# Building constants from the identity on VectorE, and turning x of one more batch on TensorE, in a fused attention and wave-MLP kernel

## The chip, the cores and the metric

The kernel runs on one core of a Trainium2 chip. A core has a matrix engine (TensorE, PE in the profile; its weight loads are shown apart as PEld), a vector engine (VectorE, DVE), a scalar engine (ScalarE, ACT), a pool engine (GpSimd, POOL) and a sync engine (SyncE, SP) that here only issues DMAs. Sixteen DMA engines move data between the memories. TensorE writes into PSUM, which has eight banks of 128 partitions by 512 float32; the other data lie in SBUF. Each engine runs its own instructions in order and waits for the others at semaphores. The metric is the device time of one execution in microseconds (us).

## The reference

Inputs are q, k and v of shape (8 batches, 8 heads, 576 positions, 64), and four weight matrices. Attention is computed twice, once on means of four positions and once in a narrow band; both are added, the heads are put side by side as x, and x goes through a wave MLP:

```python
q_d, k_d, v_d = (t.reshape(B, H, 144, 4, D).mean(axis=3) for t in (q, k, v))
out_up = np.repeat(softmax(q_d @ k_d.T / 8) @ v_d, 4, axis=2)
mask = np.abs(pos[:, None] - pos[None, :]) < 4
out_local = softmax(where(mask, q @ k.T / 8, -1e9)) @ v
x = (out_up + out_local).transpose(0, 2, 1, 3).reshape(8, 576, 512)

theta = x @ w_theta
y = w_tok_r @ (x * cos(theta)) + w_tok_i @ (x * sin(theta))
u = x + y
return u + relu(u @ w_ch)
```

## The kernel before

The work of a batch is cut into some forty small steps, each a Python generator, and the string `ORDER` names by one letter which step is emitted next; every engine runs its instructions exactly in that order. `BANKS` gives the PSUM bank of each TensorE step that writes one, and `ENGINES` says for five kinds of copies which engine makes each: p is POOL, v is VectorE, a is ScalarE. The order interleaves batches, so that the attention of one runs beside the MLP of an earlier one.

A batch goes through these steps (the letters are those of `ORDER`). **Inputs:** L loads k, q and v from SP into float32 staging tiles `st` (lines 217 and 220; thirteen items per batch, fifteen tiles in rotation); C casts them to bf16, on the engine that `ENGINES` names (line 124, as for all such copies). **Turns:** A turns k and q on TensorE (L287), a copies the result out of PSUM; d and e sum four positions of k and of q (L304; L316 on VectorE for batch 0, L321 and L322 on POOL for the others). **Pooled attention:** P scores (L369, L381), p their exponential (L388), U the pooled v as a matrix product with the pooling matrices `PU` (L335, L337), u its copy out, x spreads the last pooled rows over heads by the owner columns `own` (L350, on POOL), N the product with v (L401, L407), n its normalisation, Q and q its turn. **Band attention:** S scores (L455), s their exponential (L467), m the product with the 0-1 matrix `band` (L475, VectorE), O the product with v (L487), o and i its normalisation. **x:** T turns and t adds both attentions to x, with positions along the free axis (`xT`, L550). **MLP:** H and G multiply by the theta weights (L565, L583), h and g take sine and cosine on ScalarE (L572, L573, L590); X turns x on TensorE (L617) so that y can multiply it with sine and cosine (L633); J is the token mix (L658) with its residual j; K the channel product (L701) with its relu b; D the store.

Three parts matter for what follows.

**Constants** (step k, lines 144 to 193). The identity `ident` is made on POOL by a memset and an affine select. The matrices `band` (128 x 64), `pu0`, `pu1`, `pu4` (128 x 32 each) and `own` (128 x 4) are made on POOL too. `halves` fills a scratch tile with the value, cuts it by affine selects (two to four for each half of the partitions) and copies each half to its place.

**Weights** (step l). Twenty DMAs issued by POOL bring the weights and convert them to bf16 on the way: four pieces of theta (L251), six pieces each of the two token matrices (L249), four pieces of the channel matrix. V turns the token matrices on TensorE (L263) and v copies them out. The first mix of batch 0 needs all of them turned.

**x for the product.** In most batches X turns a batch's x by sixteen 128 x 128 transposes on TensorE into four PSUM banks, and y reads it from there. For the batches in `BY_QUEUE` (5, 6, 7) step M has SP issue two DMA transposes from SBUF to SBUF instead (L626); y then reads x from SBUF. In those batches `xT` is laid out in two separate parts, and the last piece of t is two instructions.

## Time and profile before

| | |
|---|---|
| runs shown | 236.91, 240.9 and 241.18 us; median 240.9 |
| the profiled execution | 238.6 us; span of its instructions 236.9 us |
| granted TensorE clock, mean | 0.997 |
| TensorE busy | 209.1 us, 88% of the span |
| VectorE busy | 195.1 us, 82% |
| ScalarE busy | 152.2 us, 64% |
| GpSimd busy | 90.5 us, 38% |
| moved by DMA | 49.05 MB, mean 207 GB/s |

The span runs from the first to the last instruction. An engine is busy while one of its instructions runs, whatever that instruction is worth; matmuls overlap one another, so a busy TensorE can still have slack. In a view by groups a row reads: line, engine, operation, what is written and read, shapes and count, then total and mean time, then idle time before them and what ended it. In a view by time a row begins with the start and the length in microseconds. In a row of waits three numbers follow the waiting instruction and its releaser: total, count and longest.

### The profile page before, as it was taken

What the parts mean: (1) busy time and instruction counts of PE and PEld (TensorE: products, weight loads), DVE (VectorE), ACT (ScalarE), POOL (GpSimd) and SP (SyncE); (2) the same over time, 40 slices, a digit from 0 to 9 for tenths busy, and PEclk for the clock granted to TensorE, in tenths of its full rate; (3) what the DMA queues carried; (4) which work ended last, traced back from release to release, by engine and by line L of the source; (5) the groups of instructions that cost most, each with busy time, mean ns of one, the idle gap of its engine ahead of it and who ended that gap; (6) DMA issues with size and microseconds to landing.
All of it is one profiled execution on the core that took longest, in us unless ns stands there. A gap on an engine that the chain in (4) does not pass through costs nothing.

```text
span 236.9 us, 8056 instructions
## 1 busy us (share of the span) xinstructions
PE 209.1 (88%) x3292; PEld 133.1 (56%) x3328; DVE 195.1 (82%) x386; ACT 152.2 (64%) x220; POOL 90.5 (38%) x167
## 2 busy tenths in 40 slices
PE   0543878789999999999999999999999999999993
PEld 0341754576778465665765555755755565446441
DVE  2893599797999989999989789989989899737463
ACT  2484779899987999957489987656488106331000
POOL 4880489966446456633640625343050000000000
PEclk9999999999999999999999999999999999999998
DMA  6999989998998999998999999796957276654767
GB/s 193 287 200 284 265 151 315 263 165 193 312 154 204 222 215 201 250 320 180 277 233 256 217 189 222 208 248 134 249 115 217 69 161 140 181 127 106 163 137 259
DMA packets 89174, 49.05 MB, mean 207 GB/s; under 512 B 74032, under 2 KB 76464, under 8 KB 89136
## 3 DMA queue, kind: packets, MB, share of 16 engines
q1 hardware_dynamic: 86128, 45.37, 83.2%
q0 software_dynamic: 2496, 2.38, 6.5%
q10 hardware_dynamic: 512, 0.79, 1.0%
q8 instruction: 26, 0.43, 0.8%
q14 instruction: 12, 0.10, 0.2%
HBM read 34.11 MB, written 9.44 MB: 184 GB/s over the span
## 4 chain that ended last, share of the span: by engine, by line
PE 64%; DMA 12%; DVE 10%; issue 3%; SPq 3%; POOL 3%; ACT 2%; DVEq 0%; POOLq 0%
PE space L658 26%; PE space L701 11%; PE space L565 9%; DMA st<-in_q_dram 6%; PE space L287 3%; PE space L527 3%; SPq L217 3%; DMA st<-in_v_dram 3%; DMA uT<-in_moe_w_tok_i_dram 3%; PE space L487 2%; PE space L617 2%; DVE xd L422 2%; PE space L707 1%; PE space L455 1%; PE space L583 1%
## 5 line engine op out<-in xcount | busy, mean ns | idle before, releaser
L658 PE MATMUL space<-WT,z 128*128 128x64 bf16 (+2 forms) x565 | 74.5, 284 | 0.7 <-issue 0.3
L658 PEld LDWEIGHTS <-z 128*128 128x128 bf16 x576 | 38.6, 98 | 28.8 <-issue 0.3
L674 DVE TENSOR_TENSOR uT<-space,xT 128x512 bf16<-128x512 f32 (+2 forms) x36 | 22.3, 623 | 12.8 <-PE space L658 11.7
L565 PE MATMUL space<-wth,xT 128*128 128x512 bf16 x116 | 31.0, 379 | 1.1 <-issue 0.5
L701 PE MATMUL space<-wch,uT 128*128 128x512 bf16 (+1 forms) x120 | 30.3, 372 | 0.7 <-issue 0.2
L572 ACT ACTIVATE cs<-space,pihc 128x512 bf16<-128x512 f32 x32 | 22.3, 696 | 13.0 <-PE space L565 8.4
L507 DVE TENSOR_TENSOR tmp<-space,rl 128x512 bf16<-128x512 f32 x40 | 27.1, 685 | 0.6
L550 DVE TENSOR_TENSOR xT<-space,xdT 128x464 bf16<-128x464 f32 (+3 forms) x43 | 24.5, 591 | 1.7 <-PE space L527 0.9
L467 ACT ACTIVATE pm<-space 128x1024 bf16<-128x1024 f32 (+1 forms) x24 | 20.7, 881 | 3.8 <-PE space L455 3.5
L124 ACT COPY qT<-space 128x1152 bf16<-128x1152 bf16 x15 | 16.8, 1120 | 7.9 <-PE space L287 6.6
L304 DVE TENSOR_REDUCE kd<-kT 128x290 bf16<-128x1160 bf16 x16 | 21.4, 1351 | 0.1
L715 DVE SCALAR_TENSOR_TENSOR osb<-space,ur 128x512 f32<-128x512 f32 x28 | 18.7, 682 | 2.3 <-PE space L701 2.3
L350 POOL TENSOR_TENSOR vd<-last,own 128x256 bf16<-128x256 bf16 x16 | 10.3, 651 | 25.9 <-ACT last L124 13.2
L321 POOL TENSOR_TENSOR two<-qT 128x576 f32<-128x576 bf16 x14 | 16.2, 1160 | 9.4 <-ACT qT L124 9.0
L287 PE MATMUL space<-ident,k_tm 128*128 128x128 bf16 x144 | 12.6, 242 | 7.8 <-DVE k_tm L124 6.3
L573 ACT ACTIVATE cs<-space 128x512 bf16<-128x512 f32 x32 | 19.3, 603 | 0.0
L124 POOL CAST k_tm<-st 128x576 bf16<-128x576 f32 x16 | 11.1, 700 | 21.1 <-DMA st<-in_k_dram 21.0
L124 ACT COPY kT<-space 128x1152 bf16<-128x1152 bf16 x11 | 12.3, 1119 | 9.8 <-PE space L287 7.1
L701 PEld LDWEIGHTS <-uT 128*128 128x128 bf16 x132 | 12.0, 98 | 11.4 <-issue 0.2
L124 POOL CAST v_w<-st 128x512 bf16<-128x512 f32 x22 | 13.8, 637 | 11.7 <-DMA st<-in_v_dram 9.4
L124 POOL CAST q_tm<-st 128x576 bf16<-128x576 f32 x18 | 11.9, 672 | 13.4 <-DMA st<-in_q_dram 13.4
L565 PEld LDWEIGHTS <-xT 128*128 128x128 bf16 x128 | 11.0, 98 | 10.3 <-DVE xT L550 0.4
(92 smaller groups left out, 383.1 us busy)
## 6 DMA issues: line engine op xcount, KB each, us to landing
st<-in_v_dram SPq DMA_DIRECT2D x80, 128.0 KB, 5.4
st<-in_k_dram SPq DMA_DIRECT2D x32, 288.0 KB, 5.4
st<-in_q_dram SPq DMA_DIRECT2D x32, 288.0 KB, 5.2
out_dram<-osb SPq DMA_DIRECT2D x28, 256.0 KB, 3.5
out_dram<-osb SPq DMA_DIRECT2D x6, 128.0 KB, 2.4
uT<-in_moe_w_tok_r_dram POOLq DMA_DIRECT2D x6, 108.0 KB, 7.3
uT<-in_moe_w_tok_i_dram POOLq DMA_DIRECT2D x6, 108.0 KB, 5.0
wth<-in_moe_w_theta_dram POOLq DMA_DIRECT2D x4, 128.0 KB, 5.8
```

What stands on the lines that cost most here:

```text
L124: copies[next(engines[step])](**operands)
L287: nc.tensor.transpose(out=ps[:, P * r:P * r + P], in_=(k_tm if what == "k" else q_tm)[:, i, r, :, :], identity=ident)
L304: nc.vector.tensor_reduce(out=kd[:, hs, :, 0:PG].rearrange("p e g m -> p (e g) m"), axis=AX.X, op=ALU.add, in_=kT[:, hs, :].rearrange("p e ...
L467: nc.scalar.activation(out=pm.rearrange("p e c j w -> p e (c j w)"), in_=held.pop(("S", b, u))[:, :, 0:4 * W * n], func=AF.Exp, scale=SCL)
L507: nc.vector.tensor_tensor(out=tmp.rearrange("p g (j d) -> p g j d", d=D), in0=held.pop(("loc", b, c))[:, :, :, 0:D], in1=rls.pop((b, c)).u ...
L550: nc.vector.tensor_tensor(out=xTs[b][i][:, :, lo:lo + n].rearrange("p e (m j) -> p e m j", j=4), in0=ps[:, :, at:at + n].rearrange("p e (m ...
L565: nc.tensor.matmul(out=th, lhsT=xT[:, dc, P * c:P * c + P], rhs=wth[:, dc, :], start=(dc == 0), stop=(dc == 3))
L572: nc.scalar.activation(out=cs[:, 0, :], in_=th, func=AF.Sin, bias=pihc, scale=1.0)
L573: nc.scalar.activation(out=cs[:, 1, :], in_=th, func=AF.Sin, bias=0.0, scale=1.0)
L658: nc.tensor.matmul(out=ps[:, n * i:n * i + n], lhsT=z[:, j, P * d:P * d + P], rhs=WT[:, j, lo:lo + n], start=(j == 0), stop=(j == 8))
L674: nc.vector.tensor_tensor(out=uT[:, dc, lo:lo + m], in0=ps[:, 0:m], in1=xT[:, dc, lo:lo + m], op=ALU.add)
L701: nc.tensor.matmul(out=ps, lhsT=uT[:, dc, P * c:P * c + P], rhs=wch[:, dc, cols], start=(dc == 0), stop=(dc == 3))
```

## The change

Four things change.

**The constants.** `band`, the pooling matrices and `own` no longer come from POOL. `band_of_seven` adds the two halves of the identity side by side into a padded tile and takes a running sum of seven neighbouring columns by doubling, five adds on VectorE. `means` builds a pooling matrix from a quarter of the identity by sums of four neighbouring columns, with one special column where the two blocks meet, three sums per matrix. `own` is one sum over 32 columns. POOL keeps the identity alone.

**Batch 5.** `BY_QUEUE` becomes `[6, 7]`: x of batch 5 is turned on TensorE (sixteen transposes, four bank uses) and the two DMA transposes of that batch go.

**The order and the banks.** All of `ORDER` and `BANKS` is new. The sequence of the first 36 loads on SP is the same. On POOL the casts of batch 0 now follow the identity at once, and the first weight load comes behind the cast of batch 1's second k; the second to fourth theta loads come behind both x steps of batch 0. On ScalarE the cast of batch 0's last v stands ahead of the second score exponential. The alternations between exponential and sine on ScalarE, counted in the order, are 14 instead of 18.

**The engines of copies.** Of 104 casts POOL makes 55 (56 before), ScalarE 37 (34), VectorE 12 (14); of batch 0's thirteen, POOL makes seven (one before), ScalarE four (six), VectorE two (six). Of 32 turn copies VectorE makes three (six before).

```diff
-BY_QUEUE = [5, 6, 7]
+BY_QUEUE = [6, 7]
...
-        "LkLCkLCLkALLkkaLkLCCkkLLACCdCCaklCALLAaaLedSLLLCkeLSsLPsmLCmPCLLOLLCpCLlolliOklkpolLLCLUuSAuiOLCoiLx"
+        "kkLkLLCkkkLCLCCALCACALkCaLCAaakkkaeLSLLkkLCLsdCLSCCdeLmPLpLLCLCOLLoOCLLUluusPSpsALxCoiCxNLmCinnNaLnl"
...
-    def halves(t, n, val, cuts):
-        full = rot("full", [P, 2, W], BF16, 2)
-        nc.gpsimd.memset(full, val)
-        for g in range(2):
-            for base, col, row in cuts[g]:
-                select(full[:, g, 0:n], ALU.is_ge, 0.0, base - W * g * row, [[col, n]], row)
-        for g in range(2):
-            nc.gpsimd.tensor_copy(out=t[W * g:W * g + W, :], in_=full[W * g:W * g + W, g, 0:n])
+    def add(out, a, b):
+        nc.vector.tensor_tensor(out=out, in0=a, in1=b, op=ALU.add)
+
+    def sums(out, cols, axis=AX.X):
+        with nc.allow_low_precision(reason="sums of at most one entry that is not zero"):
+            nc.vector.tensor_reduce(out=out, axis=axis, in_=cols, op=ALU.add)
+
+    def band_of_seven():
+        one_, two_, four, six = [tile_of(f"near{n}", [P, W + 7 - n]) for n in (1, 2, 4, 6)]
+        nc.vector.memset(one_, 0.0)
+        add(one_[:, 3:3 + W], identw[:, 0, :], identw[:, 1, :])
+        add(two_, one_[:, 0:W + 5], one_[:, 1:W + 6])
+        add(four, two_[:, 0:W + 3], two_[:, 2:W + 5])
+        add(six, four[:, 0:W + 1], two_[:, 4:W + 5])
+        add(band, six[:, 0:W], one_[:, 6:6 + W])
+
+    def means(t, c):
+        nc.vector.memset(t, 0.0)
+        a, b = CH * c - W0[2 * c], W + CH * c - W0[2 * c + 1]
+        n = (OWN[2 * c] + OWN[2 * c + 1]) // 4
+        sums(t[:, 0:14], quarter[:, a:a + 56].rearrange("p (m j) -> p m j", j=4))
+        at, gap = a + 56, b - a + 2
+        sums(t[:, 14:15], quarter[:, at:at + 2 * gap].rearrange("p (u g x) -> p u g x", u=1, g=2)[:, :, :, 0:2], AX.XY)
+        sums(t[:, 15:n], quarter[:, b + 60:b + 4 * n].rearrange("p (m j) -> p m j", j=4))
...
-        halves(band, W, 1.0, [[(3, -1, 1), (3, 1, -1)]] * 2)
-        yield
-        for c, r in zip((0, 1, 4), PU3):
...
-            halves(r, KP, 0.25, cuts)
-            yield
-        nc.gpsimd.memset(own, 1.0)
-        select(own, ALU.is_ge, 0.0, 0, [[-KP, 4]], 1)
-        select(own, ALU.is_ge, 0.0, KP - 1, [[KP, 4]], -1)
+        band_of_seven()
+        yield
+        nc.vector.tensor_scalar_mul(out=quarter, in0=ident, scalar1=0.25)
+        for c, t in zip((0, 1, 4), PU3):
+            means(t, c)
+            yield
+        sums(own, ident.rearrange("p (c j) -> p c j", j=KP))
         yield
```

More of the change, by code (lines that the diff above doesn't have):

```diff
@@ L66 @@
     ORDER = (
-        "LkLCkLCLkALLkkaLkLCCkkLLACCdCCaklCALLAaaLedSLLLCkeLSsLPsmLCmPCLLOLLCpCLlolliOklkpolLLCLUuSAuiOLCoiLx"
-        "CsaxLNnCACaTmCndACLNLanAnOLoaQLiqtTlSleetSCsCdVOTvoHimsPXOTpthClOolmLHLhtlHioXiSOChlTyotCUuluyCGCsPx"
-        "iVvVpxXyAaVHvVvCmNNngCCAnCnVvVhnvCOALlClZlTCavzQAoiOaTqLVtVaoTvtSSLvitCTVHvLTHtVsstVvLVHhVvVLGvgvvXV"
-        "LLXmvhyHyCddXVhVXJJLJvejJXLvyhjLeyPCSjjZmyCUJuujspJCmjLCOCOoPCLlxopCCJixCijAAaNCznANLnaeAnaOnOQLLLLL"
-        "oaiLLqoJeiTjCTtLSTTCstttSsHChORSHJddJCojihPCsmURjLCmXCCACTLpatJmCjALuClyLAdHluLOaLadPJxoLCpiOxjoHlLG"
@@ L72 @@
-        "hXiCgyeANCZnaNKhOneSXsCCLLnznoJiLCKbyjDPOpoPbLiKLTpbOLSoCUKsuQimTXqCyJTuCtCCAJbjAtatOmCSLxjHLCTLosix"
-        "JaACtCTDdJthXmLaNjCNjAyaCnJnCHOLCnOjnXQLhGooTiHCqiLgOyORTLoHLthCLCRtKThitAZoLDXiKHKaCLXThRybTbtUDytS"
-        "euKRHeGCLsLuHCbxmghCzHDxbKAACaKbdJhaCbPhjSODZopXJLyXAsaiXLyCKSjOLLyPsComLCbpmLJiLCSSzNCdsLJCCdRAnjnC"
-        "DsaNDjXJnUnLyODeOQLjTuqooKuiTCOiRexSsLtTtKLbKmtbbAFoaiCJLCePOpoPDErxTpJCjLmNHLiNnChCtLnLTLjnHthCJdMn"
-        "ADCaAjGaJDQFJgCdqjCRDmOOUHjTououihHZiMThOoiztxSYKKebEstbORPPoppHrSixySymDsKDyTsTyNTntYnhbDJNtKmnJnbj"
@@ L77 @@
-        "QJOtOjDoMqRoODJjiiJoijMmKTObOjtHoKGiDoygTKTHFiThRhHtZKyTbKtthEtyHzyKGbbDJDHhHMbJgbjJZJDjDhMhzjRHJjyh"
-        "yyjyRKrDKJYJJbjDJbjjJFDjjREKKrKbbKKKRRYDDbDKbDbbDbDD"
+        "kkLkLLCkkkLCLCCALCACALkCaLCAaakkkaeLSLLkkLCLsdCLSCCdeLmPLpLLCLCOLLoOCLLUluusPSpsALxCoiCxNLmCinnNaLnl"
+        "nAllCClCdlLLAALLamaCaQeeTOOqdCooilitSLTtLLOPsLpoPTpmTliSCtHTCCUllstthuOHuoXmhXHlyOliyoOxxhVCHoiNhiCA"
+        "CNlnvGnnCXnyCalAgOVQoVaTiqvVSvTCvtAstaCmCZVAHVVaOvovSVTLvsLTivetStXTlXytHVsHGlmVvHVvVhzLyLvhVvLLVgXe"
@@ new lines @@
+        "hVVLvvVvVJdjLyLLLLhJJCvCvLOvljOSJLmjoloCdsCCiCJilJjUOLjuuPPLpZCoClxziJmjxjpACXNaNyLLAnnCCCnOLXJanLyA"
+        "QoiCATjaaTqTKtSRtOetLSCRoLiHsdHCTLTttJLsmGXHLhCLLChmCgXHCjyhydKLCUAJhuaujbSOeJobxOsPiCpdCCoPKxpANjbC"
+        "CKLaCnXAiLnZACabaCLNeJyOCLnzneOSsdojJiQoTXCjSLCqLiUyustmJmPOCmOoLjioLuCLLpLJACCLTJxiaLCSCPjtsjpAmLCC"
+        "dxAaANLaTLnJOtnLRaSjDOoioRsJDCjLCNCnCFTiKCntULSLusTQuDmtHqOOToiHKTohLhiCDGtTHgbCLKtXexdxhAHHyZLatXhC"
+        "HCbyThACTtLXKzthLLXLGRbyCXeHXyJDgyadChACbXAyjJyaCPSaOjLsJoimRLjHpmOOLeoPLCCoiDhpLLZKidJKDbSSODjbCsKs"
@@ L79 @@
+        "mLNJNCbnConXCiAznaynEUejODLrTQuKuTxqLJoitPbtLSTtRLHTsCjpTCOPpxHoChDARtDiNaDKCCthCLCnJGXHLLbYnHLdDyeC"
+        "JjhjNFXygnnKbKXAamJyjhQXyTCAKJbqZabEjdSstOzoiJRePrpOoSijmJsmTCOPtYCUJuuoiOjmDORpSxojJToixTsNimRjttHn"
+        "hTKtNnDJOnnOQbjqGoToHHhigitTOOKhtMTHhoRZbtMoiDiHyHTtEyKTtFKDDbyHKhHMMGbhyzKKhhJDybJyDgDJyJZjjKybrJbj"
+        "jzJJRjYjbJRKDEDjJJKFDjrKbRYjjKKDbbRbKRDbDKDbKKDDbDbbDD"
     )
     BANKS = (
-        "0246024602456042604624162470236405625306245243016345062056045260154205674654235402154127056325604325"
@@ L82 @@
-        "0264602460246760217462074564230560472064016246124067204672045601423406241042501624016402316427016407"
-        "6234501643501264326403236014260462146023146023406524634602450264350645230624532406523046240367401467"
-        "62406324506324501467352415670321567567401013254765"
+        "0246024604524264026450264026542675021045602346032406723041602145620456023450267561345613520462102314"
+        "6034260246706245760247012312457032412470246247620472046745260164206142604260146204106724516245672310"
@@ L85 @@
+        "7421732461726301243604261062416720462706245607236240376304240637456203745276012576247042670423720467"
+        "243016042671061420176017451236540165231023672453245107"
     )
@@ L87 @@
         C=(
-            "pvavvvaaavavavpapaavpppppppppappppppppapppaaappapvvppavppaappppaapappavvpppapppaaappppppaaapppav"
-            "appaappa"
-        ),
-        a="aavaaaaavaaavaaaaaaaaavaaavaaaav",
-        q="avavaava",
-        u="avvvvvaaaavaaaav",
-        v="avavavvaavavvvvvaa",
+            "vvpppappapapavppvaaapvppppppppppppappppppapapappapvappappppppaapaaavvpapppapaapavvaapappaaapapaa"
+            "vpaavpaa"
+        ),
+        a="aaaaaaaaaavaaaaavaaaaaaaaaaaaava",
+        q="avvavaaa",
+        u="vvvvavvaaaavvava",
+        v="avaavaavvvvavvvava",
     )
@@ L141 @@
     own = tile_of("own", [P, 4])
+    quarter = tile_of("quarter", [P, P])
     scraps = {f: tile_of(f"scrap{i}", [P, 1], FP32) for i, f in enumerate((AF.Sin, AF.Exp))}
@@ L176, in constants @@
             yield
-        halves(band, W, 1.0, [[(3, -1, 1), (3, 1, -1)]] * 2)
+        band_of_seven()
         yield
-        for c, r in zip((0, 1, 4), PU3):
-            cuts = []
-            for blk in (2 * c, 2 * c + 1):
-                lo, n = W0[blk] - CH * c, STEP * blk - W0[blk]
-                cuts.append([(lo, -4, 1), (3 - lo, 4, -1)])
-                if n:
-                    cuts[-1].append((-n, 0, 1))
-                if n + OWN[blk] < W:
-                    cuts[-1].append((n + OWN[blk] - 1, 0, -1))
-            halves(r, KP, 0.25, cuts)
+        nc.vector.tensor_scalar_mul(out=quarter, in0=ident, scalar1=0.25)
+        for c, t in zip((0, 1, 4), PU3):
+            means(t, c)
             yield
-        nc.gpsimd.memset(own, 1.0)
-        select(own, ALU.is_ge, 0.0, 0, [[-KP, 4]], 1)
-        select(own, ALU.is_ge, 0.0, KP - 1, [[KP, 4]], -1)
+        sums(own, ident.rearrange("p (c j) -> p c j", j=KP))
         yield
```

## The prediction

> **What bounds the kernel now.** I read the stretches of the span first, because one total hides a kernel with a start and a steady part. The columns are stretch, length, then busy time of matrix engine (PE), its weight load (PEld), vector (DVE), scalar (ACT) and pool engine (POOL), granted clock, DMA share, GB/s.

> ```profile
> 18.00:24.00 6.00, 1.93 (x64) 1.05 (x56) 2.31 (x5) 2.54 (x4) 0.00 (x0) 1.00 1.12 294
> 36.00:48.00 12.00, 9.78 (x185) 6.36 (x185) 10.73 (x23) 10.94 (x17) 11.09 (x20) 1.00 1.14 287
> 48.00:60.00 12.00, 11.28 (x241) 8.66 (x242) 10.46 (x27) 11.87 (x18) 7.61 (x11) 1.00 0.97 183
> 60.00:90.00 30.00, 29.27 (x493) 20.42 (x498) 28.79 (x56) 26.84 (x39) 15.48 (x23) 1.00 1.02 223
> ```

> From 60 us on PE is covered (29.27 of 30); what it is spared or given there counts nearly whole. At 18 to 24 us every engine is idle most of the time while DMA is full (share 1.12): the start is bound by transfers. At 36 to 60 us PE has holes and ACT is nearly full (10.94 and 11.87 of 12). So I followed the chain of waits through the first 62 us.

> ```profile
> 14.23 6.49 DMA st<-in_v_dram
> ...
> 20.78 9.55 DMA st<-in_q_dram
> ...
> 30.38 0.66 POOL q_tm L124
> ...
> 38.54 6.38 DMA uT<-in_moe_w_tok_i_dram
> ...
> 60.69 1.35 PE space L658 x11
> ```

> Until 30.3 us the chain is input transfers and their issue: batch 0's last v, then batch 1's last q. Then it goes through POOL to a token-weight load, and reaches the first mix (L658) at 60.7 us. Two things can therefore shorten the kernel: inputs that land sooner, and less work on the engines that fill 36 to 60 us.

> **The change, part by part.**

> *POOL's constants and the weight loads.* POOL now builds band, pooling matrices and owner columns from 4.33 us to 17.3 us, and six weight loads are issued between them. Start, length, what:

> ```profile
> 4.33 0.20 POOL L149 MEMSET full<- 128x128 bf16 x1
> ...
> 12.01 1.61 POOL L251 DMA_DIRECT2D wth<-in_moe_w_theta_dram  x3
> ...
> 17.28 0.51 POOL L249 DMA_DIRECT2D uT<-in_moe_w_tok_r_dram  x1
> 24.06 0.66 POOL L124 CAST k_tm<-st 128x576 bf16<-128x576 f32 x1 [6.26 <-DMA st<-in_k_dram]
> ...
> 26.46 0.61 POOL L350 TENSOR_TENSOR vd<-last,own 128x256 bf16<-128x256 bf16 x1
> ```

> In the new order all that stands ahead of POOL's casts is the identity, it takes seven casts of batch 0 (one before), and the first weight load comes only behind the cast of batch 1's second k, which waits for its landing (24.06 here). The removed building was in nobody's way by itself; what matters is that six weight transfers leave the crowded stretch. Their share there, queue by queue, for 9 to 17 us and then 17 to 22 us:

> ```profile
> q1 hardware_dynamic: 4085, 1.11, 94.5%
> q0 software_dynamic: 493, 0.46, 38.3%
> ```
> ```profile
> q1 hardware_dynamic: 1530, 1.12, 93.1%
> q0 software_dynamic: 185, 0.17, 20.7%
> ```

> q0 is the weights: 0.383 x 8 + 0.207 x 5 = 4.1 us of all sixteen engines. That is the upper bound of what the inputs can win. The lower is zero, if issue sets the pace. Between them stands the issue of ten v loads, alongside the weights and, late in the kernel, without:

> ```profile
> 4.79 10.19 SPq L217 DMA_DIRECT2D st<-in_v_dram  x10
> ```
> ```profile
> 128.33 7.96 SPq L217 DMA_DIRECT2D st<-in_v_dram  x10
> ```

> 10.19 - 7.96 = 2.2 us, nearest to the case itself; to it comes a little of the 1.0 us share behind 17 us, cut because the displaced loads return at about 24 us beside batch 1's v. I take **-2.5 us** on the landing of everything from batch 0's v to batch 1's q (bounds 0 and -4.1).

> *The constants on DVE.* Twenty instructions are added: five adds and a memset for the band, one scaling, for three pooling matrices a memset and three sums each, one sum for the owners. The nearest rows:

> ```profile
> L475 DVE TENSOR_TENSOR pm<-pm,band 128x1024 bf16<-128x1024 bf16 x16 | 11.2, 707 | 0.0
> L475 DVE TENSOR_TENSOR pm<-pm,band 128x512 bf16<-128x512 bf16 x8 | 3.7, 462 | 0.0
> L304 DVE TENSOR_REDUCE kd<-kT 128x290 bf16<-128x1160 bf16 x16 | 21.4, 1351 | 0.1
> L124 DVE CAST k_tm<-st 128x576 bf16<-128x576 f32 x6 | 4.4, 748 | 7.4 <-DMA st<-in_k_dram 7.4
> L124 DVE CAST v_w<-st 128x512 bf16<-128x512 f32 x4 | 1.8, 452 | 0.0
> L169 DVE MEMSET v_w<- 128x40 bf16 x2 | 0.2, 92 | 0.2
> L124 DVE COPY kT<-space 128x1152 bf16<-128x1152 bf16 x5 | 6.7, 1349 | 0.0
> ```

> Two adds give 0.48 ns per element, so 64 columns cost about 0.25 us. A sum runs at 1.16 ns per element; over 56 columns that is 0.07 us and a fixed part, 0.2 us at a guess between 0.07 and 0.25. Together 5 x 0.25 + 0.25 + 10 x 0.2 + 4 x 0.09 = 3.9 us (bounds 20 x 0.09 = 1.8 and 20 x 0.25 = 5.0). In exchange DVE sheds of batch 0 a turn copy (1.35), two casts of k or q (0.75 each) and two of v (0.45 each), 3.7 us. The cover is that balance, and the wait for the query turn that precedes the first query sum. Were it gone, up to 3.9 us would stand ahead of key sums, pooled scores and all behind them. I count zero (bounds -1 and +1.3).

> *Waits that the order adds.* ACT now has the cast of batch 0's last v ahead of its second score exponential, second pooled exponential and third score exponential; they wait with it for the landing. PE holds the same pooled-v product ahead of them, so nothing new is late; the price is in the -2.5. PE's first turn waits for two casts in a row on DVE where one was on POOL, some 0.75 us later; ACT, which empties that turn, casts k's last piece first, so I price it at zero. On SP two transposes of x leave; in the list of waits none of PE's behind 60 us names a DMA, so they earn nothing.

> *Table switches.* ACT reloads its table whenever sine follows exponential or the reverse. Counted in the order string, the alternations fall from 18 to 14, and those ahead of the first mix from five to three.

> ```profile
> L572 ACT ACT_TABLE_LOAD x7 | 9.0, 1283 | 0.8 <-DVE osb L715 0.7
> ```

> Two loads are 2.57 us in the very stretch where ACT is full. But DVE and POOL are nearly as full there, and the last weight loads hold the same mix. I credit half, **-1.3 us** (bounds 0 and -2.6). The two saved later find ACT with slack.

> *Batch 5 on PE.* Sixteen 128x128 transposes are added where PE is covered. A group of four, and all eighty of today:

> ```profile
> 58.37 0.39 PE L617 MATMUL space<-ident,xT 128*128 128x128 bf16 x4
> ```
> ```profile
> L617 PE MATMUL space<-ident,xT x80: 216/219/230, 36.7 to 149.1; 128*128 128x128 bf16 x80
> ...
> ```

> One lasts 219 ns, but four take 0.39, so each follows the last after (0.39 - 0.219) / 3 = 0.057 us. 16 x 0.057 = **+0.9 us**; unpipelined it would be 16 x 0.219 = 3.5. The products then read x from PSUM instead of SBUF, at no cost:

> ```profile
> L633 DVE TENSOR_TENSOR z<-space,cs 128x1024 bf16<-128x1024 bf16 x20 | 13.7, 684 | 1.1 <-PE space L617 0.9
> ...
> L633 DVE TENSOR_TENSOR z<-k_tm,cs 128x1024 bf16<-128x1024 bf16 x12 | 7.8, 682 | 0.2 <-ACT cs L573 0.2
> ```

> [...] DVE's band adds have both inputs in SBUF, and POOL will be casting beside them. Today, mask products of that kind run beside casts of v:

> ```profile
> 35.85 2.22 POOL L124 CAST v_w<-st 128x512 bf16<-128x512 f32 x3
> ...
> 50.69 0.61 POOL L124 CAST v_w<-st 128x512 bf16<-128x512 f32 x1 [0.45 <-DMA st<-in_v_dram]
> ```
> ```profile
> 36.92 0.68 DVE L475 TENSOR_TENSOR pm<-pm,band 128x1024 bf16<-128x1024 bf16 x1
> ```

> The casts stretch to 0.74 each from 0.61; the product, at 0.68, is below its mean of 0.71. [...]

> *The remaining order* past the first mix I price at zero: DVE sheds two more turn copies and ACT takes them, inside a stretch that PE covers (bounds -2 and +2).

> Sum: -2.5 - 1.3 + 0.9 = -2.9 us. The profiled execution took 238.6 us, its span and 1.7 around it:

> ```profile
> span 236.9 us, 8056 instructions
> ```

> That leaves 235.7. It lay 2.3 below the median of the runs, 240.9; on the scale of the median I forecast **238.0**, 1.2% faster.

> **The rivals** (own time, then with the 2.3).

> *The start pays in full.* The transfers give back all 4.1, ACT truly binds to the first mix (-2.6), and DVE's shed copies close some of PE's holes later (-1): 238.6 - 7.7 + 0.9 = 231.8, so 234.1. For it: DMA full at 18 to 24 us, ACT 11.87 of 12. Against: the loads must be moved anyway, before the same first mix.

> *Weights come late; slower.* The last three theta loads now queue on POOL behind the two owner products of batch 0. In the trace the second ends at 27.07; 2.5 earlier, plus 1.6 for three issues, plus 5.8 to landing, gives 32.0. The first theta product needs them:

> ```profile
> 35.47 1.02 PE L565 MATMUL space<-wth,xT 128*128 128x512 bf16 x4
> ...
> ```
> ```profile
> POOL vd L350 <- ACT last L124: 13.2, 4, 7.2
> ```
> ```profile
> wth<-in_moe_w_theta_dram POOLq DMA_DIRECT2D x4, 128.0 KB, 5.8
> ...
> uT<-in_moe_w_tok_r_dram POOLq DMA_DIRECT2D x6, 108.0 KB, 7.3
> ```

> With 2.5 gained that is due at 33.0: the cover has shrunk from 16 us (13.6 + 5.8 against 35.5) to 1.0. If the owner product waits 7.2, as its longest wait here, and a landing takes 7.3, it is due at 26.2 + 7.2 + 7.3 = 40.7: 5.2 later than now, and PE, in order, stops behind it. 238.6 + 5.2 + 0.9 = 244.7, so 247.0. It eats into the gain from 1.0 us of slip and exceeds 2% from about 7.4. Against: all these waits of POOL lie behind 60 us, where it has little else to do.

> [...]

> *The start does not move,* because issue sets the pace: 238.6 + 0.9 = 239.5, so 241.8.

> **How the numbers follow.** Forecast 0.45, full pay 0.28, late weights 0.12, start unmoved 0.10, port 0.05. Runs of this kernel spread over 1.8% (236.91 to 241.18), so 2%, 4.8 us, is about what can be told from no change. Full pay is faster beyond it: 0.28. Late weights are slower beyond it: 0.12. The other three lie within: 0.60. The range runs from a full pay with a little of the order's -2 (234.1 - 1.6) to an unmoved start with the transposes at 3.5 instead of 0.9 (241.8 + 2.6): 232.5 to 244.4; it leaves out most of late weights. The likeliest case alone spans 235 to 241.

> **What would show it.** Right: the last q of batch 1 lands near 27.8 instead of 30.3; q0 is nearly empty until 20 us; the first mix starts at 56 to 58; fourteen table loads; 96 transposes of x, four still in 0.39. Wrong: PE waiting on the theta weights at all, a v issue that still takes 10 us, DVE adds above 0.6 us, or the holes of PE behind 60 us growing by more than 2 us, which would make the order, not the start, the story.

## The result and the profile after

| | before | after |
|---|---|---|
| median of six runs, us | 237.65 | 234.78 |
| lowest to highest | 236.91 to 241.18 | 234.07 to 238.07 |
| the profiled execution, and its span | 238.6, 236.9 | 234.87, 233.0 |
| cast of the last q of batch 1 begins | 30.38 | 26.41 |
| first theta product begins | 35.47 | 34.67 |
| first mix begins | 60.53 | 56.73 |
| from there to the end of the span | 176.34 | 176.26 |
| matmul, vector, scalar, pool engine busy | 209.1, 195.1, 152.2, 90.5 | 210.3, 196.1, 149.9, 83.1 |

The ratio of after to before is 0.9881, with a 95% interval of 0.9834 to 0.9928: 1.2% faster, less than the 2% called a difference in the prediction. The ratios here and below leave out executions of both kernels that ran disturbed (among them the profiled executions of e9, e10 and e12 below, and eight of e10's thirteen, which took 242.9 to 245.6 us), so that a ratio can differ from that of two medians.

The two spans differ by 3.9 us, and the first mix comes 3.8 earlier; behind it the two kernels take equally long. So the change decides in the first 57 us. The same stretches as before (stretch, length, busy time of PE, PEld, DVE, ACT, POOL, clock, DMA share, GB/s):

```profile
18.00:24.00 6.00, 4.88 (x90) 3.50 (x90) 4.42 (x9) 4.50 (x7) 3.10 (x6) 1.00 1.06 343
36.00:48.00 12.00, 11.52 (x220) 8.54 (x222) 10.86 (x25) 10.84 (x18) 10.74 (x18) 0.93 1.15 286
48.00:60.00 12.00, 11.67 (x206) 8.40 (x205) 10.98 (x25) 11.93 (x22) 6.45 (x11) 1.00 0.86 164
60.00:90.00 30.00, 29.63 (x514) 19.86 (x517) 28.24 (x56) 23.31 (x34) 17.49 (x26) 1.00 1.00 244
```

PE works 4.88 us at 18 to 24 us instead of 1.93, and 11.52 instead of 9.78 at 36 to 48: the hole of the start is smaller. ACT is as full as before ahead of the mix (11.93 of 12). The chain of waits of the changed kernel, up to the first mix:

```profile
15.36 5.46 DMA st<-in_k_dram
20.84 6.93 DMA st<-in_v_dram
27.80 0.33 DVE kd L314
28.13 1.02 DVE pm L485
...
34.74 1.82 PE space L575 x4
...
55.35 0.51 PE space L273 x12
55.86 0.30 PE space L627 x4
56.16 0.63 PE space L273 x15
56.80 3.41 PE space L668 x27
```

The inputs set the pace to 27.8 us instead of 30.4. Then comes VectorE (lines of DVE) instead of POOL, and at the end the turns of the token weights (L273) and the mix on PE itself. The theta product at 34.74 is on the chain, but 4.0 us won on the landing of the last q have become 0.8 us there. The first mix nevertheless wins 3.8: something other than the landing helped. One candidate shows in the chain of the kernel before, which runs through ScalarE from 52.86 us to shortly before the mix and has two table loads in it:

```profile
53.60 1.28 ACT L467 ACT_TABLE_LOAD   x1
...
57.15 1.28 ACT L572 ACT_TABLE_LOAD   x1
```

The chain of the changed kernel has no table load in it.

### The profile page after: what moved, and what is told of

The parts are those of the page before. It is cut to its first block, busy times and chain, and to the rows that moved or that the text cites. A ratio compares the mean times of both kernels' runs of the same rounds, so it can differ in the third digit from the quotient of the medians.

```text
span 233.0 us, 8062 instructions
## 1 busy us (share of the span) xinstructions
PE 210.3 (90%) x3309; PEld 134.1 (58%) x3344; DVE 196.1 (84%) x402; ACT 149.9 (64%) x220; POOL 83.1 (36%) x125
## 4 chain that ended last, share of the span: by engine, by line
PE 78%; DMA 8%; DVE 7%; SPq 4%; issue 2%; ACT 0%; DVEq 0%; ACTq 0%
PE space L668 30%; PE space L711 12%; PE space L575 11%; PE space L297 4%; PE space L537 3%; DMA st<-in_v_dram 3%; SPq L227 3%; PE space L497 3%; DMA st<-in_q_dram 2%; PE space L465 2%; DMA st<-in_k_dram 2%; PE space L627 2%; DVE tmp L517 2%; PE space L717 1%; PE space L411 1%
## 5 line engine op out<-in xcount | busy, mean ns | idle before, releaser
L711 PE MATMUL space<-wch,uT 128*128 128x512 bf16 (+1 forms) x125 | 31.2, 373 | 0.4
L331 POOL TENSOR_TENSOR two<-qT 128x576 f32<-128x576 bf16 x14 | 17.2, 1229 | 20.8 <-ACT qT L124 20.6
L314 DVE TENSOR_REDUCE kd<-kT 128x290 bf16<-128x1160 bf16 x16 | 21.5, 1349 | 0.0
L124 POOL CAST q_tm<-st 128x576 bf16<-128x576 f32 x20 | 13.5, 677 | 18.8 <-DMA st<-in_q_dram 18.8
L124 ACT COPY qT<-space 128x1152 bf16<-128x1152 bf16 x16 | 18.0, 1127 | 1.3 <-PE space L297 0.9
L124 POOL CAST v_w<-st 128x512 bf16<-128x512 f32 x19 | 12.6, 664 | 17.5 <-DMA st<-in_v_dram 13.4
L124 POOL CAST k_tm<-st 128x576 bf16<-128x576 f32 x16 | 11.2, 702 | 19.2 <-DMA st<-in_k_dram 19.0
L124 ACT COPY kT<-space 128x1152 bf16<-128x1152 bf16 x13 | 14.6, 1124 | 5.1 <-PE space L297 5.1
L575 PEld LDWEIGHTS <-xT 128*128 128x128 bf16 x128 | 11.5, 99 | 10.3 <-issue 0.5
L485 DVE TENSOR_TENSOR pm<-pm,band 128x1024 bf16<-128x1024 bf16 (+1 forms) x24 | 16.4, 693 | 1.0 <-ACT pm L477 1.0
## 6 DMA issues: line engine op xcount, KB each, us to landing
st<-in_v_dram SPq DMA_DIRECT2D x80, 128.0 KB, 5.1
out_dram<-osb SPq DMA_DIRECT2D x6, 128.0 KB, 3.4
uT<-in_moe_w_tok_r_dram POOLq DMA_DIRECT2D x6, 108.0 KB, 6.6
uT<-in_moe_w_tok_i_dram POOLq DMA_DIRECT2D x6, 108.0 KB, 5.5
wth<-in_moe_w_theta_dram POOLq DMA_DIRECT2D x4, 128.0 KB, 6.5
```

The lines of the kernel that those rows point to most:

```text
L124: copies[next(engines[step])](**operands)
L314: nc.vector.tensor_reduce(out=kd[:, hs, :, 0:PG].rearrange("p e g m -> p (e g) m"), axis=AX.X, op=ALU.add, in_=kT[:, hs, :].rearrange("p e ...
L575: nc.tensor.matmul(out=th, lhsT=xT[:, dc, P * c:P * c + P], rhs=wth[:, dc, :], start=(dc == 0), stop=(dc == 3))
L711: nc.tensor.matmul(out=ps, lhsT=uT[:, dc, P * c:P * c + P], rhs=wch[:, dc, cols], start=(dc == 0), stop=(dc == 3))
```

## The experiments

Twelve kernels were run, each timed beside the kernel before. Letters are steps of `ORDER`; of that string only the stretch in question is shown. The times in the last three columns come from one profiled execution each. There the first mix differs by 3 us between kernels of about equal ratio (the changed kernel, e7 and e9), so the ratio decides, and the profile says where to look.

| run | ratio to before, 95% interval | last q of batch 1 is cast | first mix | from there |
|---|---|---|---|---|
| after | 0.9881, 0.9834 to 0.9928 | 26.41 | 56.73 | 176.3 |
| e1 weights early in after | 0.9916, 0.9883 to 0.9949 | 27.59 | 57.52 | 177.4 |
| e2 weights late in before | 1.0043, 1.0003 to 1.0082 | 26.10 | 59.90 | 176.4 |
| e3 two more table loads | 1.0011, 0.9975 to 1.0047 | 25.37 | 59.57 | 176.6 |
| e4 x turned twice | 1.0131, 1.0056 to 1.0205 | 25.74 | 60.19 | 181.2 |
| e5 VectorE constants in before | 1.0011, 0.9973 to 1.0048 | 29.37 | 59.54 | 177.6 |
| e6 POOL constants in after | 0.9984, 0.9946 to 1.0023 | 30.16 | 60.73 | 177.6 |
| e7 constants first | 0.9883, 0.9820 to 0.9946 | 26.15 | 59.57 | 176.5 |
| e8 batch 5 by queue again | 0.9864, 0.9802 to 0.9926 | 25.56 | 56.04 | 178.4 |
| e9 two sines | 0.9906, 0.9868 to 0.9944 | 26.36 | 59.99 | 176.4 |
| e10 e2 and e5 together | 1.0047, 0.9990 to 1.0104 | 27.25 | 65.04 | 176.6 |
| e11 e7, theta early | 0.9954, 0.9921 to 0.9986 | 29.24 | 58.88 | 176.3 |
| e12 holes filled | 0.9892, 0.9818 to 0.9965 | 25.65 | 57.14 | 178.6 |

Differences between two runs in us are differences of their ratios times 238.

**e1: the weights back in the crowd.** The changed kernel, six weight loads (l) moved forward again.

```diff
-"kkLkLLCkkkLCLCCALCACALkCaLCAaakkkaeLSLLkkLCLsdCLSCCdeLmPLpLLCLCOLLoOCLLUluus"
+"kkLkLLCkkkLCLCClALCACALkCaLClllAaakkkaeLSLLkkLCLsdClLSCCldeLmPLpLLCLCOLLoOCLLUuus"
```

> The changed kernel with the first six weight loads issued again at about 8.5 to 17 us, between POOL's casts of batch 0, as before the change; all else as changed. Theory (the gain of the start is transfer time that these loads no longer take): the last q of batch 1 is cast near 30 instead of 26.4, the first mix starts at 59 to 60 instead of 56.7, the time comes back by 2 to 3.5 us, ratio to the kernel before 0.996 to 1.003. Rival (the start gained by the shorter POOL queue and the shed work on VectorE, not by DMA): last q within 0.5 us of 26.4, ratio within 0.003 of 0.988.

Measured: 0.9916, between the two expectations. The landing is later by 1.2 us, with a wait of 2.5 at the last q:

```profile
27.59 0.66 POOL L124 CAST q_tm<-st 128x576 bf16<-128x576 f32 x1 [2.52 <-DMA st<-in_q_dram]
```

That costs 0.0035, 0.8 us, with an interval from -0.5 to 2.2. The transfers carry less of the gain than was put down for them.

**e2: the weights late in the old order.** The other way round: the kernel before, its first six weight loads moved to where the changed kernel has them.

```diff
-"CCaklCALLAaaLedSLLLCkeLSsLPsmLCmPCLLOLLCpCLlolliOklkpolLLCLUuSAuiOLCoiLxCsaxLNnCACaTmCndACLN"
+"CCakCALLAaaLedSLLLCkeLSsLPsmLCmPCLLOLLCpCLoiOkkpoLLClLUuSAuiOLCoiLxCsaxllllLNnCACaTmCndAClLN"
```

> The kernel before, with its first six weight loads moved behind the cast of batch 1's second k and the owner products, where the changed kernel has them; nothing else moved. Theory (DMA): the last q of batch 1 is cast near 27 instead of 30.4 and the first mix starts 2 to 3 us earlier than 60.6, ratio 0.987 to 0.992. Rival (it takes the new order to use it): the q lands earlier but POOL's longer queue of weight loads and the token weights hold the first mix, which stays at 60 to 61; ratio 0.997 to 1.003.

Measured: 1.0043, no gain at all, though the last q came 4.3 us earlier than before. What took it, on PE (start, length, what, and in brackets the idle time before it and what ended that):

```profile
31.76 0.22 PE L263 MATMUL space<-ident,uT 96*128 96x96 bf16 x1 [2.03 <-DMA uT<-in_moe_w_tok_r_dram]
32.75 0.26 PE L263 MATMUL space<-ident,uT 96*128 96x96 bf16 x1 [0.78 <-DMA uT<-in_moe_w_tok_r_dram]
33.23 0.26 PE L263 MATMUL space<-ident,uT 96*128 96x96 bf16 x1 [0.22 <-DMA uT<-in_moe_w_tok_r_dram]
...
34.15 1.91 PE L565 MATMUL space<-wth,xT 128*128 128x512 bf16 x4
```

PE waits 3.0 us for token weights that are now late (0.8 at this place before), and the theta product behind them begins only 1.3 us earlier than before. Here PE reaches the turn of these weights (V) at 29.7 us, ahead of its first theta product; the new order puts it behind the third. Behind these waits the clock column reads 0.50 from 32.0 to 38.9 us, which it doesn't in the kernel before; what that adds isn't separated. In this order, at least, the earlier landing is spent on waiting for the weights that were displaced.

**e3 and e9: what a table load costs.** In the changed kernel a tiny exponential and a tiny sine (step 2 and step 1, one column each into a scrap tile) stand ahead of g, so that ScalarE loads two more tables; in e9 two tiny sines stand there, which need no load (e9 has 14 loads, as the changed kernel).

```diff
-"CXnyCalAgOVQoVaT"
+"CXnyCalA21gOVQoVaT"
```

> The changed kernel with one tiny exponential and one tiny sine put ahead of batch 0's tail sine on ScalarE: two more table loads ahead of the first mix, as in the kernel before, some 2.9 us of ScalarE time. As forecast (half of a table load is on the path): first mix 1.3 to 1.6 us later than 56.7, ratio 0.993 to 0.995. Rival one (ScalarE binds): 2.6 to 3 us later, ratio about 1.000. Rival two (ScalarE has slack there): less than 0.4 us later, ratio 0.987 to 0.990.

```diff
-"CXnyCalAgOVQoVaT"
+"CXnyCalA11gOVQoVaT"
```

> The changed kernel with two tiny sines (128x1 each) instead of the tiny exponential and sine of the earlier run, at the same place on ScalarE: the same two extra instructions, but no table load beside the fourteen. Theory, the loads themselves cost: 2 x 0.20 us at the most, ratio 0.987 to 0.991. Rival, any extra instruction at that place breaks the sequence there: ratio above 0.996, as with the two loads (1.0011).

Measured: 1.0011 with the loads, 0.9906 without them. ScalarE's row of e3:

```profile
43.47 1.28 ACT L207 ACT_TABLE_LOAD   x1
44.76 0.20 ACT L207 ACTIVATE scrap<-pihc 128x1 f32<-128x1 f32 x1
44.97 1.28 ACT L207 ACT_TABLE_LOAD   x1
46.26 0.20 ACT L207 ACTIVATE scrap<-pihc 128x1 f32<-128x1 f32 x1
```

The two loads alone cost 0.0105, 2.5 us; they last 2 x 1.28 = 2.56. (Both intervals together allow 1.3 to 3.7.) The two extra instructions cost 0.6, with an interval that takes in zero and 2.0. The best estimate is that a table load costs its whole length at this place. The late first mix of e9's profiled execution, 59.99, isn't borne out by its ratio.

**e4: the price of a transpose.** The changed kernel turns each of the 96 pieces of x twice.

```diff
-            for dc in range(4):
+            for dc in (0, 1, 2, 3, 0, 1, 2, 3):
                 nc.tensor.transpose(...)
```

> The changed kernel with every x that TensorE turns (batches 0 to 5) turned twice into the same place: 96 more transposes, six times what the change adds. Theory (57 ns each and covered by nothing): 96 x 0.057 = 5.5 us, ratio 1.011; it would put the change's own sixteen at 0.9 us. Rival one (219 ns each): 21 us, ratio 1.08. Rival two (TensorE's holes take them): under 2.5 us, ratio below 0.999.

Measured: 1.0131, which is 0.0250 or 5.9 us above the change: 0.062 us for each of 96 (0.040 to 0.084 by both intervals). Eight in a row take 0.61 in the profile, so a step of (0.61 - 0.219) / 7 = 0.056, though the mean of one alone is 227 ns:

```profile
L627 PE MATMUL space<-ident,xT 128*128 128x128 bf16 x192 | 15.3, 227 | 0.0
...
70.62 0.61 PE L627 MATMUL space<-ident,xT 128*128 128x128 bf16 x8
```

So the price of a transpose here isn't its duration, 0.227 us, but about the distance to the next one, 0.056.

**e5, e6 and e10: the constants.** e5 has the old order and takes only the constants from VectorE; e6 has the new order and the constants from POOL.

```diff
-        band_of_seven()
+        halves(band, W, 1.0, [[(3, -1, 1), (3, 1, -1)]] * 2)
...
-            means(t, c)
+            halves(r, KP, 0.25, cuts)
...
-        sums(own, ident.rearrange("p (c j) -> p c j", j=KP))
+        nc.gpsimd.memset(own, 1.0)
+        select(own, ALU.is_ge, 0.0, 0, [[-KP, 4]], 1)
+        select(own, ALU.is_ge, 0.0, KP - 1, [[KP, 4]], -1)
```

(That is e6; e5 is its reverse, in the kernel before.)

> The kernel before with the constants alone built on VectorE from the identity; order, banks, engines of copies and batch 5 as before. POOL then issues its first weight loads at about 4.5 us. Theory (the constants gain only with an order that uses the freed POOL; here VectorE gets 3 to 4 us more ahead of batch 0's sums): first mix 1 to 3 us later than 60.5, ratio 1.004 to 1.012. Rival (the constants are the change's gain by themselves): first mix before 59, ratio below 0.995.

> The changed kernel with the constants built on POOL as before; all else as changed. POOL then builds for some 10 us between its casts of batch 0, and the casts of v's second and fourth piece come at about 22 us instead of 14 and 16. Theory: pooled v of batch 0 moves from 19.3 to about 23 us and the first mix 2.5 to 4 us later than 56.7, ratio 0.999 to 1.005: the VectorE constants are what lets the order start so. Rival (ScalarE's table loads are the gain and the start has room): first mix under 1 us later, ratio below 0.993.

Measured: 1.0011 for e5, so neither gain nor loss in the old order, where a loss was expected; 0.9984 for e6, 0.0103 or 2.4 us above the change (1.0 to 3.9). In e6 POOL builds until 22.9 us, and the casts of batch 0's v stand behind that; PE waits for one of them:

```profile
22.86 1.17 POOL L124 CAST v_w<-st 128x512 bf16<-128x512 f32 x2
```
```profile
23.52 0.44 PE L516 MATMUL space<-v_w,pm 64*64 64x65 bf16 x16 [5.38 <-POOL v_w L124]
```

So the constants earn nothing by themselves, but the new order loses without them, for it gives POOL seven of batch 0's casts. e10 puts e2 and e5 together, to see whether each was only the other's missing cover:

> The kernel before with both halves of the new start at once: the first six weight loads moved late and the constants built on VectorE; its order is otherwise the old one, with eighteen table loads. Theory, the start pays only with the table loads gone and with an order made for it: no gain, ratio 0.996 to 1.004. Rival, the two halves were each the other's missing cover (alone they gave 1.0043 and 1.0011): ratio 0.988 to 0.993.

Measured: 1.0047, no gain. PE again waits for token weights, 1.4, 1.0 and 0.7 us. The parts don't pay in the old order, singly or together.

**e7 and e11: an earlier start still.** In e7 VectorE builds all constants at the very front, right behind the identity; its fills of other tiles follow, and batch 0's first key sum (d) comes ahead of its first query sum (e).

```diff
-"kCaLCAaakkkaeLSLLkkLCLsdCLSCC"
+"kCaLCAaakkkadeLSLLkkLCLsCLSCC"
...
         nc.vector.memset(pihc, PIH)
+        band_of_seven()
+        nc.vector.tensor_scalar_mul(out=quarter, in0=ident, scalar1=0.25)
+        for c, t in zip((0, 1, 4), PU3):
+            means(t, c)
+        sums(own, ident.rearrange("p (c j) -> p c j", j=KP))
         yield
```

> The changed kernel with the constants at the very front of VectorE, while it waits for the first k and POOL is idle, the zero and one fills behind the casts of k instead, and batch 0's first key sum ahead of its first query sum. Expected: the band's adds take 0.2 us each instead of up to 0.6 beside POOL's casts; batch 0's pooled scores end at about 16.5 instead of 18.3 us. If VectorE binds the start, the first mix comes 1 to 2 us earlier, ratio 0.980 to 0.984; if transfers or ScalarE bind, under 0.5 us and ratio 0.986 to 0.989.

Measured: 0.9883, as the change. The pooled v of batch 0 came 2.3 us earlier (17.04 instead of 19.31), but that of batch 1 waited for its last v:

```profile
38.81 0.29 PE L347 MATMUL space<-v_w,pu 128*32 128x128 bf16 x4 [2.15 <-POOL v_w L124]
```

The weight loads that left the first 22 us run beside just these loads. So e11 put the four theta loads of e7 (l) back to 9 to 17 us:

```diff
-"LkCaLCAaakkkadeLSLLkkLCLsCLSCCdeLmPLpLLCLCOLLoOCLLUluus"
+"LkCaLClAaakkkadeLSLLkkLCLsCLSCCllldeLmPLpLLCLCOLLoOCLLUuus"
```

> The earlier variant of the changed kernel with the constants at the very front and the first key sum ahead of the first query sum, and now the four theta loads issued at 9 to 17 us again (the first behind the cast of batch 0's last q, three behind its fourth v). If batch 1's last v, at 38 us there, was held by the weight loads at 24 to 36 us, it lands 1 to 2 us earlier and the first mix comes at 55 to 57: ratio 0.978 to 0.986. If the transfers only move the jam forward, ratio 0.986 to 0.992, as with the six early loads (0.9916).

Measured: 0.9954, outside both expectations. POOL no longer waits for batch 1's v, but its last q is cast at 29.24, 3.1 us later than in e7. Early loads hold the inputs, late ones hold the v of batch 1: they were moved, not saved.

**e8: batch 5 back on the queue.** The changed kernel with x of batch 5 turned by two DMA transposes, its products a few steps later, and sixteen PE transposes less, their four uses of `BANKS` with them.

```diff
-BY_QUEUE = [6, 7]
+BY_QUEUE = [5, 6, 7]
-"DKCCthCLCnJGXHLLbYnHLdDyeCJjhjNFXygnnKbKXAamJyjh"
+"DKCCtMMhCLCnJGHLLbYnHLdDeCJjhjNFgnnKbKAamyJjyh"
```

> The changed kernel with x of batch 5 turned by two DMA transposes again, issued as soon as x is there, its four products moved a few steps later on VectorE to leave the transposes time, and the sixteen transposes on TensorE gone. Theory (TensorE is covered there and each transpose costs 57 ns): 0.9 us faster than the changed kernel, ratio about 0.984. Rival (turning on TensorE pays, since the transposes by DMA hold back the mix or other transfers): slower than the changed kernel, ratio above 0.990.

Measured: 0.9864, 0.4 us below the change, with an interval of 0.0062 each way: it doesn't tell the two expectations apart.

**e12: holes of PE filled.** Looking for what eats the earlier landing, the clock stood out: in the changed kernel's profiled execution it falls at 34 us, and the first four theta products take 1.89 us where the kernel before needs 1.02. e12 puts matmuls of no use into the holes ahead of it; each writes a bank that the following turn overwrites.

```diff
+FILL = {(0, 0): 12, (0, 1): 22}
...
             tmp = tmps.pop((b, c))
+            for f in range(FILL.get((b, c), 0)):
+                nc.tensor.matmul(out=ps[:, f % 4, :], lhsT=ident, rhs=ident, start=True, stop=True)
```

> The changed kernel with 34 matmuls of the identity on itself (128x128) put into holes of PE between 28 and 32 us: 12 ahead of batch 0's first turn of x, 22 ahead of the second, each into the bank that the turn then overwrites. In the profile of the changed kernel the granted clock falls to 0.50 from about 34 to 38 us, behind a hole of 1.6 us, and the first four theta products take 1.89 us instead of 1.03. Theory, that drop takes back a part of the earlier start: with the hole filled the clock stays at 1.00 up to the first mix, the first theta products take about 1.03, the first mix comes at 55 to 56, ratio 0.980 to 0.986. Rival, VectorE sets that stretch: the clock stays up, and the ratio is that of the change, 0.986 to 0.991. If the drop comes all the same, the hole was not its cause. The fill costs PE 34 x 0.056 = 1.9 us, of it 0.7 outside the holes.

Measured: 0.9892, and the clock fell all the same. First the changed kernel by windows, then e12 (PE busy is the first number behind the length, the clock the third from the end), then PE's rows of e12:

```profile
30.00:34.00 4.00, 1.94 (x59) 1.44 (x52) 4.00 (x9) 1.98 (x4) 3.42 (x6) 1.00 1.23 175
34.00:38.00 4.00, 3.99 (x68) 1.97 (x67) 3.08 (x6) 3.71 (x6) 2.74 (x5) 0.57 1.07 265
38.00:42.00 4.00, 3.79 (x62) 2.36 (x65) 3.88 (x11) 2.88 (x6) 4.00 (x8) 1.00 1.05 365
```
```profile
30.00:34.00 4.00, 2.66 (x99) 2.30 (x96) 4.00 (x9) 1.71 (x3) 3.10 (x7) 1.00 0.92 145
34.00:38.00 4.00, 3.91 (x53) 1.72 (x39) 3.25 (x8) 3.65 (x5) 2.85 (x6) 0.57 1.06 317
```
```profile
29.41 1.39 PE L535 MATMUL space<-ident 128*128 128x128 bf16 x22
30.64 0.37 PE L540 MATMUL space<-ident,tmp 128*128 128x116 bf16 x4
32.18 0.32 PE L498 MATMUL space<-v_w,pm 64*64 64x65 bf16 x16 [1.18 <-DVE tmp L518]
...
34.23 1.86 PE L578 MATMUL space<-wth,xT 128*128 128x512 bf16 x4
```

The fill shortened the holes between 30 and 34 us from 2.06 to 1.34 us; 1.18 of that is one wait for VectorE, which was busy for all of these 4 us in both kernels. The clock still falls, so either the rest is enough for it or the hole isn't the cause; the count in the last section speaks for the first. What the fall costs in time isn't separated by any experiment. One pair of profiles bears on it: e8 has the same instructions up to the first mix and no fall, and its first mix begins 30.5 us after the cast of the last q, against 30.3 in the changed kernel. So no cost shows there, though e8 has waits of its own, 1.45 us for a cast of v and 0.68 for a token weight.

## Why the prediction came out

The forecast was 238.0 us on the scale of a median of 240.9, which is 1.2% faster; measured is 1.2%, between 0.7 and 1.7. In absolute time 234.78 is 3.2 us below the forecast: the six runs of the kernel before have a median of 237.65, so the 2.3 us that were added for the scale didn't hold. What came out is the case that it held likeliest, and the sum up to the first mix, -2.5 - 1.3 = -3.8 us, is what the profile shows there. But the terms behind that sum were sized wrongly, in opposite directions, so that the agreement of the sum is in part luck.

**The transfers, -2.5 us: too large.** The landing itself won even more, 4.0 us, and q0 is empty where it was to be: at 9 to 17 us the changed kernel lists the input queue alone. But the reasoning by which 2.5 was chosen failed: ten v loads should issue faster without the weights, and still take almost 10 us, which the prediction named as a sign that it is wrong.

```profile
4.78 9.87 SPq L227 DMA_DIRECT2D st<-in_v_dram  x10
```
```profile
q1 hardware_dynamic: 4998, 1.40, 91.4%
```

In 8 us q1 now moves 1.40 MB instead of 1.11: the weights had taken bandwidth, not SP's issue. And the prediction let the landing pass on to the first mix, cutting only a little for the displaced loads. They return in full. The queues at 24 to 36 us, before and after:

```profile
q1 hardware_dynamic: 5379, 2.17, 84.9%
q0 software_dynamic: 226, 0.22, 15.1%
```
```profile
q1 hardware_dynamic: 4879, 1.34, 68.2%
q0 software_dynamic: 1002, 0.95, 56.3%
```

Moving the weights back costs 0.8 us (e1), moving them alone gains nothing (e2, e10). The rival of weights that come late, with its small cover, is real in the old order, as PE's waits in e2 show. In the changed kernel's profile PE waits for no weight ahead of the first mix; but the cover is thin, for in e8 and e12, whose order is the same up to there, it waits 0.68 and 0.34 us for a token weight at about 44 us.

**The table loads, half credited, -1.3 us: probably too small.** Fourteen are left, as counted. Their price ahead of the first mix is measured as the full length, 2.5 us for two (e3 against e9); the half lies at the lower edge of the interval. The reason given for the half, that VectorE and POOL are nearly as full there, doesn't hold at 48 to 60 us, where ScalarE has 0.07 us of 12 free and POOL works 6.45.

**The constants, zero: right alone, wrong in the order.** By themselves they earn and cost nothing (e5), as counted. Yet taken out of the new order they cost 2.4 us (e6). The prediction said that building on POOL was in nobody's way; in the new order it would be, in that of seven casts.

These undo prices, 0.8, 2.5 and 2.4, make 5.7 us with an error of some 2.3, against 3.8 gained at the first mix, so it isn't shown whether they overlap. What is shown is that a part has another worth in the new order than in the old: the constants are worth 2.4 us in the one and nothing within 0.9 in the other. The gain comes with the new order, its banks and its engines of copies; it needs the constants off POOL and two table loads fewer, and the order asks for the weights later. What each of order, banks and engines gives isn't tested.

**The band adds, 0.25 us each.** Three take 0.20, two are held. VectorE's adds, and POOL's casts beside them, in the changed kernel; then the adds of e7, where POOL stands still:

```profile
7.90 0.60 DVE L149 TENSOR_TENSOR near<-ident 128x64 bf16<-128x64 bf16 x1
8.54 0.91 DVE L149 TENSOR_TENSOR near<-near 128x69 bf16<-128x69 bf16 x2
9.48 0.20 DVE L149 TENSOR_TENSOR near<-near,near 128x65 bf16<-128x65 bf16 x1
```
```profile
7.79 0.67 POOL L124 CAST q_tm<-st 128x576 bf16<-128x576 f32 x1 [1.01 <-DMA st<-in_q_dram]
8.50 0.67 POOL L124 CAST k_tm<-st 128x576 bf16<-128x576 f32 x1
```
```profile
1.34 0.20 DVE L149 TENSOR_TENSOR near<-ident 128x64 bf16<-128x64 bf16 x1 [0.41 <-POOL ident L146]
1.57 0.43 DVE L149 TENSOR_TENSOR near<-near 128x69 bf16<-128x69 bf16 x2
```

An add ends when the cast beside it does, at 8.5 and at 9.2 us, twice 0.4 to 0.5 us late; these casts take 0.67 us, as do those at 10.49 and 11.67 us, which have no add beside them. In the prediction's rows it was the casts that were longer beside VectorE's products, 0.74 each instead of 0.61. What decides which of the two is held, no run shows. The two held adds took 0.60 and 0.68 us, which the prediction had named as a sign of being wrong. The case that its chances name port, at 0.05, is that of adds held beside POOL's casts, and it was rightly set low: two of the five adds were held, some 0.9 us in all, and e7, which takes that away, is no faster (0.9883 against 0.9881). That all five are held, no run shows.

**Batch 5, +0.9 us: borne out** in its unit price by e4 (0.062 us instead of 0.057, with a wide interval); e8, which measures it in place, is too coarse. **The remaining order, zero:** behind the first mix the two profiles differ by 0.1 us, with the transposes in it, so the order may have won back some 0.8. One profile each can't show that: e5, with the order of the kernel before, takes 1.3 us longer behind the mix than that kernel.

What stays open is how much of the landing's 4.0 us VectorE and the clock take between 28 and 38 us.

## What to carry to other kernels

Before an earlier transfer is credited, follow the transfer that it displaces to its new place and look who waits there, for here the weights that left the first 22 us came back at 24 to 36 us, where q0 moved 0.95 MB instead of 0.22. A switch of tables on an engine that is full up to the next join can cost its whole length, as it did here by the best estimate (2.5 us for two loads of 1.28), even beside busy neighbours. A part of a reordering can be worth nothing alone and yet be needed by the whole, so the price of undoing it is not what it gives by itself.

## What had not been expected of the hardware

**TensorE ran at half its rate in the start, and the clock column doesn't show it.** Nine transposes of 128x128 in a row, in the changed kernel early and late:

```profile
7.06 1.14 PE L297 MATMUL space<-ident,k_tm 128*128 128x128 bf16 x9 [7.06 <-DVE k_tm L124]
...
26.15 1.17 PE L297 MATMUL space<-ident,k_tm 128*128 128x128 bf16 x9
```
```profile
42.13 0.67 PE L297 MATMUL space<-ident,k_tm 128*128 128x128 bf16 x9
```

1.14 against 0.67 us is a distance of about 0.11 against 0.056 between two of them, while the column says 1.00 at all three places. In some executions it is recorded, in e12 as 0.50 at 22 to 26 us. The kernel before is slow in the same way until 30 us and at full rate after that: nine of its transposes take 1.16 us at 28.65 and 0.68 at 31.10. In the profiled executions of the new order, and in e2 and e10, the clock falls to 0.50 once more, in e3, e4, e7 and e10 twice, between 28 and 60 us; in e8 it doesn't, and neither in e5 with the old order.

The recorded changes of the clock lie whole multiples of 3.41 us apart: in the changed kernel at 27.37, 34.19, 37.61 and 232.17 us (2, 1 and 57 times 3.41), in the kernel before at 30.47 and 235.27 (60 times). The second fall lasts 3.41 us in the changed kernel, from 34.2 to 37.6; in e2 and e6 it lasts 6.83 and in e9 and e11 10.24, two and three such steps. The longest wait of PE in the eight microseconds ahead of it is 1.6 us, and in e12 1.2, so the clock fell without a wait as long as a step. What ends the slow start, no run shows.

**Ten loads took 10 us to issue** at the start, without or with weights beside them (9.87 and 10.19 us), and 7.96 late in the kernel before; what holds SP there, no run shows.
